# A fused attention and feed-forward kernel: the first four attention steps take the later steps' row halves, and their loads are cut and moved

## The chip, the cores and the metric

The kernel runs on one core of one Trainium2 chip, in one launch. The metric is device time in microseconds (us), the median of several executions; lower is better. The core's engines are TensorE (PE in the rows, its weight loads PEld), VectorE (DVE), ScalarE (ACT), GpSimd (POOL) and SyncE (SP), which issues nearly all the DMAs.

## The reference

Three stages run one after the other, all in float32:

```python
# 1. decayed linear attention, 2 batches, 8 heads, 768 positions in 12 blocks of 64, head size 64
for b in range(nb):
    qb, kb, vb = q[:, :, sl], k[:, :, sl], v[:, :, sl]
    intra = einsum('bhic,bhjc->bhij', qb, kb) * Dmask        # lam ** (i - j), lower triangle
    intra = einsum('bhij,bhjd->bhid', intra, vb)
    inter = einsum('bhid,bhde->bhie', qb * lam_pow, kv_state)
    out[:, :, sl] = intra + inter
    kv_state = lam_block * kv_state + einsum('bhsd,bhse->bhde', kb * rev_pow, vb)
# 2. x (1536 x 512): h = x @ w_in (512 x 2048); g = max(0.01 h, h); x = g @ w_out (2048 x 512)
# 3. h = x @ w_in2 (512 x 1024); softmax * h; layer norm * g_ln; @ w_out2 (1024 x 512)
```

## The kernel before

**Tiles of the attention.** The 12 blocks of 64 positions are steps 0 to 11. A step handles both batches (`NB` = 2) and four pairs of heads (`NPAIR` = 4); the two heads of a pair lie on the two halves of the 128 partitions. `HALF[h]` is rows 0 to 63 or 64 to 127, and `rows(h)` is the other half. A step has four groups of 64 x 64 matrix products, 16 products each (32 MATMUL rows in the profile, two for each):

- `scores_mm` (L204): k times q, into a bank; VectorE multiplies it with a decay table (`scores_ev`, L212) and gives `r`;
- `xs_mm` (L258): v times r, the part within the block;
- `state_mm` (L218): decayed k times v, which VectorE adds to the decayed state (`state_ev`, L244);
- `xq_mm` (L272): state times scaled q, accumulated with `xs_mm` in the same bank.

Here a quarter is the pair of the row half that a product's operands lie on and the row half of the bank that its result goes to. Before, the first `NPRE` = 4 steps keep k by position (`kj`) and v with head h on `HALF[h]` (`jrows`), and the later steps on `HALF[1 - h]`. So in steps 0 to 3 `scores_mm` and `xq_mm` both read `HALF[1 - h]` and write `HALF[h]`, which are the same two quarters, while `xs_mm` and `state_mm` have four different ones. Because the two parts of an x bank come from different row halves there, step 3 marks the banks with a small product and a copy (`see`, L249 to L252) between them, and the first `xq_mm` of steps 1 and 2 waits for the state's last addition by hand.

**The front.** The program runs steps 0 to 3 alone, up to the first product of the feed-forward part (`l1_mm`, L445), while it prepares the first weights. Each weight matrix (1 MB or 0.5 MB raw per half, `IN` and `OUT`) goes through two ScalarE passes (`words`: L358 and L362), three VectorE passes (`clamp` L368, `shift` L378, `join` L387), a ScalarE copy (`high` L415) and a VectorE subtraction (`low` L434). From then on TensorE alternates `l1_mm` (L445) and `l2_mm` (L461); its first `l2_mm` takes the result of the first `l1_mm` through two ScalarE instructions (L448, L451). Step 3's state product is left for later, and is paired with step 4's scores:

```python
            if i == 5:
                both(scores_mm, NPRE, aps[0], state_mm, NPRE - 1, kb)
```

(L1008; `both` puts two groups in turn, pair of heads by pair of heads.) Steps 4 to 11 follow inside the feed-forward loop, each with `both(xs, state)` and `both(xq, next scores)`.

**What sets the order.** Every engine runs its instructions in the order in which the code issues them; the last lines of the kernel chain them so. `load(queue, out, in_, limit)` lets a DMA start only when, with it, at most `limit` bytes are under way (2 MB by default, `AHEAD`; `CALM` is 1 MB), by a wait of the issuing queue for an older DMA. A DMA also waits for the one that used its semaphore before it; there are eight of these for SP and ACT together, in turn.

## Time and profile before

| | |
|---|---|
| median of 3 runs | 424.29 us (423.1 to 426.34) |
| the profiled execution | 423.9 us |
| its span, first to last instruction | 422.0 us |
| time outside the span | 1.9 us |
| TensorE busy | 413.6 us, 98% of the span |
| instructions in the profile | 8023 |

The span is from the first to the last instruction. A busy TensorE is not a TensorE at its peak, since matmuls are pipelined and their ends modelled. "Idle before, releaser" says how long an engine stood before an instruction and what ended the wait; "issue" is a wait for nothing that the profile shows.

### The profile page before, as it was taken

The page shows a single profiled execution, that of the slowest core. Times are in us where ns is not written, and L with a number is a line of the kernel's source. Part 1 is how long each engine was busy: PE and PEld are TensorE (multiplying, and loading weights), DVE is VectorE, ACT ScalarE, POOL GpSimd, SP SyncE. Part 2 cuts the span into 40 slices and gives each one's busy share as a digit, 9 for nine tenths or more (in the row PEclk, how much of TensorE's full clock was granted, in tenths as well). Part 3 has the DMA queues.
Part 4 walks back from the last instruction along what each step waited for, and adds up shares of the span by engine and source line. Part 5 has one row for each costly group of instructions (what it writes and reads, how often), then busy time and mean ns, then how long its engine had stood idle before and what let it go on. Part 6 is the DMA issues. An engine that isn't in the chain of part 4 may idle for free.

```text
span 422.0 us, 8023 instructions
## 1 busy us (share of the span) xinstructions
PE 413.6 (98%) x3166; PEld 340.4 (81%) x3166; DVE 323.7 (77%) x465; ACT 251.4 (60%) x395; POOL 126.0 (30%) x125
## 2 busy tenths in 40 slices
PE   7899999999999999999999999999999999999997
PEld 3778788888888888888888888888878888888886
DVE  4699999989894769988986789974569897847520
ACT  3598987867734555556465367742287558465621
POOL 0600001111157346236427342008212394123100
PEclk9999999999999999999999999999999999999999
DMA  8699995597300604413403745331043543535531
GB/s 294 246 319 364 311 346 165 159 272 223 109 23 1 214 37 149 127 49 125 149 29 122 236 148 190 100 101 26 2 143 106 161 158 107 182 120 173 176 123 51
DMA packets 30373, 64.69 MB, mean 153 GB/s; under 512 B 3328, under 2 KB 12032, under 8 KB 29824
## 3 DMA queue, kind: packets, MB, share of 16 engines
q1 hardware_dynamic: 30192, 63.79, 45.8%
q8 instruction: 25, 0.41, 0.4%
q10 hardware_dynamic: 144, 0.39, 0.3%
q14 instruction: 12, 0.10, 0.1%
HBM read 49.49 MB, written 14.68 MB: 152 GB/s over the span
## 4 chain that ended last, share of the span: by engine, by line
PE 84%; DMA 1%; DVE 1%; ACT 1%; issue 0%; SPq 0%; ACTq 0%
PE acc L461 19%; PE acc L676 11%; PE hps L445 9%; PE aps L795 8%; PE aps L560 8%; PE hps L560 8%; PE hps L795 7%; PE aps L461 5%; PE hps L461 5%; PE aps L258 2%; PE aps L272 1%; DMA lt<-kept_t 1%; PE hps L204 1%; DMA kept_t<-e 1%; PE aps L218 1%; ACT xhi L645 0%
## 5 line engine op out<-in xcount | busy, mean ns | idle before, releaser
L461 PE MATMUL acc<-ghi,wio 128*128 128x512 f32 x256 | 64.0, 392 | 0.3 <-DVE wio L434 0.3
L461 PEld LDWEIGHTS acc<-ghi,wio 128*128 128x128 f32 x256 | 47.6, 188 | 10.7 <-DVE wio L434 0.7
L445 PE MATMUL hps<-xhi,wio 128*128 128x512 f32 x160 | 42.1, 394 | 0.5 <-ACT xhi L307 0.5
L795 PE MATMUL aps<-wb,ln 128*128 128x512 f32 (+1 forms) x168 | 36.5, 375 | 0.1
L509 POOL TENSOR_TENSOR sw<-wio 128x512 f32<-128x512 f32 x14 | 21.9, 1582 | 46.7 <-DVE sj L528 46.7
L943 ACT ACTIVATE tf<-tf 128x512 f32<-128x512 f32 x28 | 17.7, 632 | 29.7 <-DVE tf L1121 29.7
L445 PEld LDWEIGHTS hps<-xhi,wio 128*128 128x128 f32 x160 | 29.6, 188 | 6.9 <-ACT xhi L307 0.6
L198 POOL TENSOR_TENSOR sd<-state,masks 128x512 f32<-128x512 f32 x9 | 9.6, 1063 | 85.0 <-DVE state L233 51.1
L795 PEld LDWEIGHTS aps<-wb,ln 128*128 128x128 f32 x168 | 29.9, 188 | 6.1 <-ACT ln L777 0.5
L461 PE MATMUL acc<-glo,wio 128*128 128x512 f32 x128 | 34.2, 389 | 0.0
L795 PE MATMUL hps<-wb,ln 128*128 128x512 f32 (+1 forms) x144 | 30.6, 371 | 0.0
L795 PEld LDWEIGHTS hps<-wb,ln 128*128 128x128 f32 x144 | 25.5, 188 | 4.8
L734 ACT ACTIVATE e<-e,small 128x1024 f32<-128x1024 f32 x12 | 13.8, 1150 | 25.1 <-DVE small L728 25.0
L461 PEld LDWEIGHTS acc<-glo,wio 128*128 128x128 f32 x128 | 24.0, 188 | 5.0
L362 ACT ACTIVATE raww<-raww 128x1024 uint32<-128x1024 uint16 (+1 forms) x28 | 27.8, 994 | 0.0
L676 PE MATMUL acc<-wa,xhi 128*128 128x512 f32 x104 | 27.8, 389 | 0.0
L358 ACT ACTIVATE x<-raww 128x1024 f32<-128x1024 f32 (+1 forms) x24 | 23.3, 969 | 7.0 <-DMA raww<-in_w_in_dram 7.0
L378 DVE SCALAR_TENSOR_TENSOR raww<-x,raww 128x1024 uint32<-128x1024 uint32 (+1 forms) x24 | 24.6, 1025 | 3.2 <-ACT raww L362 2.0
L781 DVE TENSOR_TENSOR ln<-lt,ln 128x1024 fp32r<-128x1024 f32 x12 | 15.3, 1273 | 14.0 <-ACT ln L777 14.0
L1121 DVE TENSOR_TENSOR tf<-aps,tf 128x512 f32<-128x512 f32 x26 | 17.6, 688 | 10.4 <-PE aps L560 10.0
L387 DVE SCALAR_TENSOR_TENSOR x<-x,raww 128x1024 uint32<-128x1024 uint32 (+1 forms) x24 | 24.8, 1032 | 0.1
L676 PEld LDWEIGHTS acc<-wa,xhi 128*128 128x128 f32 x104 | 19.4, 188 | 4.2 <-DVE e L714 0.2
(197 smaller groups left out, 998.2 us busy)
## 6 DMA issues: line engine op xcount, KB each, us to landing
raww<-in_w_out_dram SPq DMA_DIRECT2D x23, 512.0 KB, 5.1
raww<-in_w_in_dram SPq DMA_DIRECT2D x16, 512.0 KB, 5.6
kept_t<-e SPq DMA_DIRECT2D x12, 512.0 KB, 2.6
lt<-kept_t SPq DMA_DIRECT2D x48, 128.0 KB, 3.0
qk<-in_att_dram SPq DMA_DIRECT2D x8, 512.0 KB, 5.3
raww<-in_w_in_dram SPq DMA_DIRECT2D x4, 1024.0 KB, 5.1
gk<-kept_g SPq DMA_DIRECT2D x16, 256.0 KB, 2.7
kept_g<-tf SPq DMA_DIRECT2D x14, 256.0 KB, 2.0
```

Of the source, the lines that this page charges most:

```text
L358: act.activation(x, raw[:, :, 1].bitcast(F32), AF.Copy, scale=HI_SCALE)
L362: act.activation(raw[:, :, 0], raw.bitcast(U16)[:, :, 1], AF.Copy, scale=LO_SCALE)
L378: dve.scalar_tensor_tensor(raw[:, :, 0], x.bitcast(U32), 3, raw[:, :, 0], op0=ALU.logical_shift_left, op1=ALU.bitwise_or)
L387: dve.scalar_tensor_tensor(xu, xu, 0x80000000, raw[:, :, 0], op0=ALU.bitwise_and, op1=ALU.bitwise_or)
L445: pe.matmul(bank, w[:, s, k], x[b][:, k], start=(i == 0), stop=(i == len(terms) - 1))
L461: pe.matmul(banks[m], w[:, s, m], x, start=start, stop=stop)
L509: pool.tensor_tensor(t, w[:, 0], w[:, 1], op=ALU.add)
L560: pe.matmul(bank, left_[s][j], right[r][j], start=(i == 0), stop=(i == len(terms) - 1))
L676: pe.matmul(bank, x, Bp[w, j][:, s], start=(i == 0), stop=(i == len(terms) - 1))
L795: pe.matmul(po[:, 0:n], x[:, k], w2_t["b", k][:, s, cols], start=(i == 0), stop=(i == len(terms) - 1))
L943: act.activation(t, t if src is None else src, AF.Prelu, alpha=0.01)
L1121: dve.tensor_tensor(t, banks[n], other, op=ALU.add)
```

## The change

Only the first four steps and the loads ahead of the feed-forward part change:

- `kj` and v of steps 0 to 3 go to `rows(h)`, as in the later steps. Their loads are no longer part of two wide DMAs and one DMA for v, but two DMAs of 64 partitions for v and two for kj. A step is loaded by six DMAs (256 KB, 256 KB and four of 128 KB) where it was three (384, 384 and 256 KB).
- `scores_mm` of steps 0 to 3 writes `rows(h)`. The scores of steps 2 and 3 are issued in turn with `xq_mm` of steps 1 and 2 (`both`).
- `see`, its waits and the waits for the state's addition are gone.
- One decay table where there were two, so four scans fewer on VectorE.
- Step 3's `scale_k` is on GpSimd and not on ScalarE; `words`, `high`, `clamp`, `shift` and `join` of the first output weights stand in other places between steps 2 and 3 and the first `l1_mm`.
- The limit of the first output-side loads is 1.5 MB and 1 MB where it was 1.25 MB and 0.5 MB.

The line of the pairing at i == 5 is as before.

```diff
--- before.py
+++ after.py
@@ -74,9 +74,9 @@
     xlo = [cp.tile([P, KD, NBLK], F32R, name=f"xlo{i}") for i in range(NTOK // NBLK)]
 
 
-    masks = mp.tile([P, 3, NPAIR, CH], F32, name="masks")
-    dmask, dfirst, qpow = masks[:, 0], masks[:, 1], masks[:, 2]
-    junk = masks[:, 0:2].rearrange("p n a b -> p (n a b)").bitcast(BF16)
+    masks = mp.tile([P, 2, NPAIR, CH], F32, name="masks")
+    dmask, qpow = masks[:, 0], masks[:, 1]
+    junk = masks.rearrange("p n a b -> p (n a b)").bitcast(BF16)
     kept_y = dp.tile([KD, P, NBLK], F32, name="kept_y")
     kept_t = dp.tile([NTOK // P, P, FF2], F32, name="kept_t")
     kept_g = dp.tile([NF, P, NBLK], F32, name="kept_g")
@@ -89,14 +89,6 @@
     def rows(h):
 
         return HALF[1 - h]
-
-    def jrows(s, h):
-
-        return HALF[h] if s < NPRE else HALF[1 - h]
-
-    def decay(s):
-
-        return dfirst if s < NPRE else dmask
 
     def at(bank, rows, b, pr):
 
@@ -129,15 +121,29 @@
                 break
         flight.append((ins, size))
 
+    def put_kj(t, s):
+
+        for h in range(2):
+            load(sync, out=t[rows(h)], in_=att[2 * s : 2 * s + 2, HALF[h], 2].rearrange("n p a b -> p n a b"))
+
+    def put_v(t, s):
+
+        for h in range(2):
+            load(sync, out=t[rows(h)], in_=vt[s, HALF[h]])
+
     def load_step(s):
 
         t = wp.tile([P, 2048], F32, tag="w", name="ldw")
-        qkk = t[:, 0:1536].rearrange("p (n c a b) -> p n c a b", n=NB, c=3, a=NPAIR)
-        v = t[:, 1536:2048].rearrange("p (n a b) -> p n a b", n=NB, a=NPAIR)
+        qk = t[:, 0:1024].rearrange("p (n c a b) -> p n c a b", n=NB, c=2, a=NPAIR)
+        kj, v = (t[:, o : o + 512].rearrange("p (n a b) -> p n a b", n=NB, a=NPAIR) for o in (1024, 1536))
         for b in range(NB):
-            load(act if s + b == 1 and s == 0 else sync, out=qkk[:, b], in_=att[2 * s + b])
-        load(sync, out=v, in_=vt[s])
-        ld[s] = (qkk[:, :, 0], qkk[:, :, 1], qkk[:, :, 2], v)
+            load(act if s + b == 1 and s == 0 else sync, out=qk[:, b], in_=att[2 * s + b, :, 0:2])
+        ld[s] = (qk[:, :, 0], qk[:, :, 1], kj, v)
+
+    def load_kjv(s):
+
+        put_v(ld[s][V], s)
+        put_kj(ld[s][KJ], s)
 
     BOTH = slice(0, 2)
     qk_t = {}
@@ -152,16 +158,14 @@
         if s >= NS:
             return
         kj = ap1.tile(SHAPE, F32, tag="kj", name="kj")
-        for h in range(2):
-            load(sync, out=kj[rows(h)], in_=att[2 * s : 2 * s + 2, HALF[h], 2].rearrange("n p a b -> p n a b"))
+        put_kj(kj, s)
         ld[s][KJ] = kj
 
     def load_v(s):
         if s >= NS:
             return
         v = ap2.tile(SHAPE, F32, tag="v", name="v")
-        for h in range(2):
-            load(sync, out=v[rows(h)], in_=vt[s, HALF[h]])
+        put_v(v, s)
         ld[s] = {V: v}
 
     def scale_q(s, eng):
@@ -181,7 +185,7 @@
 
         if s >= NS - 1:
             return
-        kj, last = ld[s][KJ], decay(s)
+        kj, last = ld[s][KJ], dmask
         if eng is act:
             by_pair(kj, kj, last)
         else:
@@ -201,23 +205,21 @@
         q, k = (qk_t[s][:, :, 0], qk_t[s][:, :, 1]) if s >= NPRE else ld[s][0:2]
         for h in range(2):
             d = rows(h)
-            pe.matmul(at(bank, jrows(s, h), b, pr), k[d, b, pr], q[d, b, pr], start=True, stop=True)
+            pe.matmul(at(bank, d, b, pr), k[d, b, pr], q[d, b, pr], start=True, stop=True)
 
     def scores_ev(s, bank):
         if s >= NS:
             return
         r_t[s] = ap1.tile(SHAPE, F32, tag="r", name="r")
         for src, dst in parts(bank, r_t[s]):
-            mask = decay(s) if len(src.shape) == 3 else decay(s).unsqueeze(1).to_broadcast(SHAPE)
+            mask = dmask if len(src.shape) == 3 else dmask.unsqueeze(1).to_broadcast(SHAPE)
             dve.tensor_tensor(dst, src, mask, op=ALU.mult)
 
     def state_mm(s, bank, b, pr):
 
         for h in range(2):
-            j = jrows(s, h)
-            pe.matmul(at(bank, rows(h), b, pr), ld[s][KJ][j, b, pr], ld[s][V][j, b, pr], start=True, stop=True)
-
-    added = {}
+            j = rows(h)
+            pe.matmul(at(bank, j, b, pr), ld[s][KJ][j, b, pr], ld[s][V][j, b, pr], start=True, stop=True)
 
     def state_ev(s, bank):
         if s >= NS - 1:
@@ -230,54 +232,43 @@
         if s not in sd_t:
             src = bank.rearrange("p (n a b) -> p n a b", n=NB, a=NPAIR)
             for pr in range(NPAIR):
-                ins = dve.scalar_tensor_tensor(
+                dve.scalar_tensor_tensor(
                     s_t[s + 1][:, :, pr],
                     s_t[s][:, :, pr],
                     qpow[:, pr, CH - 1 : CH],
                     src[:, :, pr],
                     op0=ALU.mult,
                     op1=ALU.add,
-                ).ins
-                added.setdefault(s, ins)
+                )
             return
         for src, dst, old in parts(bank, s_t[s + 1], sd_t[s]):
-            added[s] = dve.tensor_tensor(dst, src, old, op=ALU.add).ins
-
-    LASTPRE, seen, mark = NPRE - 1, {}, tabs[:, 0:NB]
-
-    def see(s, b):
-        c = CH - 1
-        bank = (aps, hps)[b][0]
-        pe.matmul(bank[:, 0:CH], c1.to_broadcast([P, P]), c1.to_broadcast([P, CH]), start=True, stop=True)
-        seen[b] = act.copy(mark[:, b : b + 1], bank[:, c : c + 1]).ins
+            dve.tensor_tensor(dst, src, old, op=ALU.add)
+
+    LASTPRE = NPRE - 1
 
     def xs_mm(s, bank, b, pr):
 
         for h in range(2):
-            j = jrows(s, h)
-            ins = pe.matmul(
+            j = rows(h)
+            pe.matmul(
                 at(bank, HALF[h], b, pr),
                 ld[s][V][j, b, pr],
                 r_t[s][j, b, pr],
                 start=(s == 0 or (s != LASTPRE and pr + b == 0)),
                 stop=(s == 0 or (s == LASTPRE and pr == NPAIR - 1)),
-            ).ins
-            if s == LASTPRE and pr + h == 0:
-                tc.add_manual_dep(ins, seen[b].name, SYNC, reason="another half of rows")
+            )
 
     def xq_mm(s, bank, b, pr):
 
         for h in range(2):
             d = rows(h)
-            ins = pe.matmul(
+            pe.matmul(
                 at(bank, HALF[h], b, pr),
                 s_t[s][d, b, pr],
                 qs_t[s][d, b, pr],
                 start=(s == LASTPRE and pr == 0),
                 stop=(s != LASTPRE and pr + b == NPAIR + NB - 2),
-            ).ins
-            if s < LASTPRE and pr + b + h == 0:
-                tc.add_manual_dep(ins, added[s].name, SYNC, reason="another half of rows")
+            )
 
     def each_pair(*groups):
 
@@ -812,26 +803,30 @@
 
     pool.memset(one, 1.0)
     delta = heads(tabs[:, 0:256])
-    lams = tabs[:, 256:264].rearrange("p (a b) -> p a b", a=2)
+    lams = tabs[:, 260:264]
     pool.memset(zero, 0.0)
-    def scan(table, side, first):
+    def scan(table, first):
 
         for pr in range(NPAIR):
-            lam = lams[:, side, pr : pr + 1].to_broadcast([P, CH])
+            lam = lams[:, pr : pr + 1].to_broadcast([P, CH])
             if first is None:
                 dve.tensor_tensor_scan(table[:, pr], lam, delta[:, pr], 0.0, op0=ALU.mult, op1=ALU.add)
             else:
                 dve.tensor_tensor_scan(table[:, pr], lam, zero, first, op0=ALU.mult, op1=ALU.add)
 
     load(sync, out=tabs, in_=tab)
-    scan(dfirst, 0, None)
+    scan(dmask, None)
     load_step(0)
+    load_kjv(0)
     load_weights(0, IN)
     load_step(1)
+    load_kjv(1)
     load_step(2)
+    load_kjv(2)
     load_step(3)
-    load_weights(0, OUT, 5 * CALM // 4)
-    load_weights(1, OUT, CALM // 2)
+    load_kjv(3)
+    load_weights(0, OUT, 3 * CALM // 2)
+    load_weights(1, OUT, CALM)
     load_weights(2, BOTH, CALM)
     load_weights(3)
     load_qk(NPRE)
@@ -844,8 +839,7 @@
     scale_k(0, dve)
     busy(3)
     scores_ev(0, sb[0])
-    scan(qpow, 1, 1.0)
-    scan(dmask, 1, None)
+    scan(qpow, 1.0)
     scale_q(1, pool)
     words(0, IN)
     both(xs_mm, 0, xb[0], state_mm, 0, kb)
@@ -864,42 +858,35 @@
     join(0, IN)
     scale_q(2, pool)
     scale_k(2, act)
-    alone(scores_mm, 2, sb[0])
     state_ev(1, kb)
     decay_state(2, pool)
     high(0, IN)
-    alone(xq_mm, 1, xb[1])
+    both(xq_mm, 1, xb[1], scores_mm, 2, sb[0])
     scores_ev(2, sb[0])
+    x_hi(1, xb[1])
     low(0, IN)
-    x_hi(1, xb[1])
     both(xs_mm, 2, xb[0], state_mm, 2, kb)
+    scale_q(3, pool)
+    state_ev(2, kb)
     x_lo(1, xb[1])
-    scale_q(3, pool)
-    scale_k(3, act)
-
-    alone(scores_mm, 3, sb[1])
-    state_ev(2, kb)
     decay_state(3, pool)
-    word_hi(0, OUT)
-    alone(xq_mm, 2, xb[0])
+    scale_k(3, pool)
+    both(xq_mm, 2, xb[0], scores_mm, 3, sb[1])
+    words(0, OUT)
+    x_hi(2, xb[0])
     scores_ev(3, sb[1])
     clamp(0, OUT)
     x3 = (xb[1], hps[1])
-    for b in range(NB):
-        each_pair((xq_mm, 3, x3, b))
-        see(3, b)
-        if b == 0:
-            word_lo(0, OUT)
-            shift(0, OUT)
-    x_hi(2, xb[0])
-    join(0, OUT)
+    alone(xq_mm, 3, x3)
+    shift(0, OUT)
     x_lo(2, xb[0])
     alone(xs_mm, 3, x3)
+    join(0, OUT)
     x_hi(3, x3)
+    x_lo(3, x3)
+    words(1, OUT)
     high(0, OUT)
-    x_lo(3, x3)
     low(0, OUT)
-    words(1, OUT)
     clamp(1, OUT)
     shift(1, OUT)
     words(2, IN)
```

**TensorE, steps 2 and 3 up to the first feed-forward product.** L204 is `scores_mm`, L272 `xq_mm`, L251 `see`, L258 `xs_mm`, L445 `l1_mm`. Before, from the scores of step 3:

```order
L204 MATMUL acc_87<-ldw 64x64 x16
L272 MATMUL acc_84<-qs,state 64x64 x16
L272 MATMUL acc_85<-qs,state 64x64 x8
L251 LDWEIGHTS const-bfloat16-1.0
L251 MATMUL aps_90<-const-bfloat16-1.0 128x64
L272 MATMUL hps_89<-qs,state 64x64 x8
L251 LDWEIGHTS const-bfloat16-1.0
L251 MATMUL hps_88<-const-bfloat16-1.0 128x64
L258 MATMUL acc_85<-r,ldw 64x64 x8
L258 MATMUL hps_89<-r,ldw 64x64 x8
L445 MATMUL hps_88<-xhi_97,wio 128x512 x8
```

Now the first two groups stand in turn (the first rows of eight pairs of rows), L208 being `scores_mm`, L265 `xq_mm`, L253 `xs_mm` and L436 `l1_mm`:

```order
L265 MATMUL acc_84<-qs,state 64x64 x2
L208 MATMUL acc_87<-ldw 64x64 x2
...
L265 MATMUL acc_85<-qs,state 64x64 x8
L265 MATMUL hps_89<-qs,state 64x64 x8
L253 MATMUL acc_85<-r,ldw 64x64 x8
L253 MATMUL hps_89<-r,ldw 64x64 x8
L436 MATMUL hps_88<-xhi_97,wio 128x512 x8
```

The products of scores and xq alternate by twos, and no row of `see` is left between xq and xs of step 3.

**ScalarE, around x_hi of step 3.** L307 is `x_hi` (step 2, then step 3 in two halves), L358 and L362 are `words`, L415 `high`, L448 the activation after the first `l1_mm`. Before:

```order
L252 COPY tabs<-hps_88 128x1
L307 CAST xhi_97<-acc_84 128x2x4x64
L307 CAST xhi_97<-acc_85 128x4x64
L307 CAST xhi_97<-hps_89 128x4x64
L415 CAST wio<-x 128x512
L358 ACTIVATE x<-raww 128x512
L362 ACTIVATE raww<-raww 128x512
L358 ACTIVATE x<-raww 128x512
L362 ACTIVATE raww<-raww 128x512
L415 CAST wio<-x 128x512
L448 ACTIVATE hps_88<-hps_88 128x512
```

Now, with L298 `x_hi`, L349 and L353 `words`, L406 `high` and L439 the activation:

```order
L298 CAST xhi_97<-acc_84 128x2x4x64
L298 CAST xhi_97<-acc_85 128x4x64
L298 CAST xhi_97<-hps_89 128x4x64
L349 ACTIVATE x<-raww 128x512
L353 ACTIVATE raww<-raww 128x512
L406 CAST wio<-x 128x512
L349 ACTIVATE x<-raww 128x512
L353 ACTIVATE raww<-raww 128x512
L406 CAST wio<-x 128x512
L439 ACTIVATE hps_88<-hps_88 128x512
```

The first `high` after `x_hi` stood ahead of the two `words` of the next weights, and now stands behind them.

**SP, the loads of the first two steps.** Each row is one DMA or several alike, in the order of issue. Before:

```order
L123 DMA tabs<-in_tab_dram 128x264
L123 DMA ldw<-in_att_dram 128x768
L123 DMA ldw<-in_vt_dram 128x512
L123 DMA raww<-in_w_in_dram 128x1024
L123 DMA ldw<-in_att_dram 128x768 x2
L123 DMA ldw<-in_vt_dram 128x512
```

Now:

```order
L115 DMA tabs<-in_tab_dram 128x264
L115 DMA ldw<-in_att_dram 128x512
L115 DMA ldw<-in_vt_dram 64x512 x2
L115 DMA ldw<-in_att_dram 64x2x256 x2
L115 DMA raww<-in_w_in_dram 128x1024
L115 DMA ldw<-in_att_dram 128x512 x2
L115 DMA ldw<-in_vt_dram 64x512 x2
L115 DMA ldw<-in_att_dram 64x2x256 x2
```

The bytes per step are the same; k by position, which came within the first two DMAs of a step, now comes last.

## Rows read from the trace of the kernel before

**Rows 1.** The page: busy time of each engine, its share of the span, and instructions

```profile
PE 413.6 (98%) x3166; PEld 340.4 (81%) x3166; DVE 323.7 (77%) x465; ACT 251.4 (60%) x395; POOL 126.0 (30%) x125
```

**Rows 2.** Stages: length; busy PE, PEld, DVE, ACT, POOL; granted clock; DMA share; GB/s

```profile
0.00:25.00 25.00, 20.01 (x476) 14.69 (x477) 14.94 (x33) 13.11 (x30) 7.38 (x12) 1.00 0.78 265
25.00:45.00 20.00, 20.00 (x89) 16.31 (x87) 18.78 (x33) 17.59 (x30) 0.00 (x0) 1.00 0.99 344
45.00:65.00 20.00, 19.71 (x145) 16.05 (x145) 19.64 (x23) 18.19 (x26) 0.00 (x0) 1.00 0.98 347
```

**Rows 3.** Waits of TensorE in the first 120 us: total, times, longest

```profile
PE acc L204 <- DMA ldw<-in_att_dram: 2.0, 2, 1.1
PE acc L204 <- issue: 1.7, 2, 1.5
PE acc L461 <- DVE wio L434: 0.3, 1, 0.3
```

**Rows 4.** Timeline of TensorE, steps 0 to 3: start, length, what, idle before

```profile
8.18 0.23 PE L258 MATMUL acc<-r,ldw 64*64 64x64 f32 x2
...
13.12 0.52 PE L204 MATMUL acc<-ldw 64*64 64x64 f32 x12
13.86 0.74 PE L204 MATMUL acc<-ldw 64*64 64x64 f32 x19 [0.23 <-issue]
...
16.44 0.52 PE L204 MATMUL acc<-ldw 64*64 64x64 f32 x12
18.42 0.80 PE L204 MATMUL acc<-ldw 64*64 64x64 f32 x20 [1.46 <-issue]
19.05 1.57 PE L272 MATMUL acc<-qs,state 64*64 64x64 f32 x48
20.55 0.20 PE L251 MATMUL aps<-const-bfloat16-1.0 128*128 128x64 bf16 x1
20.68 0.68 PE L272 MATMUL hps<-qs,state 64*64 64x64 f32 x16
```

**Rows 5.** The page's queue of instruction fetches: packets, MB, share

```profile
q8 instruction: 25, 0.41, 0.4%
```

**Rows 6.** Two stages of the front, columns as in Rows 2

```profile
10.00:15.00 5.00, 4.09 (x134) 3.33 (x136) 3.13 (x5) 2.54 (x9) 3.51 (x3) 1.00 0.99 359
15.00:20.00 5.00, 3.54 (x151) 3.40 (x147) 3.39 (x6) 3.06 (x8) 3.50 (x4) 1.00 0.42 142
```

**Rows 7.** TensorE: first and last of 64 rows, scores of step 4 with state of 3

```profile
45.06 0.27 PE L204 MATMUL aps<-qk 64*64 64x64 f32 x2
...
45.99 0.22 PE L218 MATMUL aps<-ldw 64*64 64x64 f32 x2
```

**Rows 8.** Timeline from the first l1_mm to the first l2_mm

```profile
23.05 2.11 PE L445 MATMUL hps<-xhi,wio 128*128 128x512 f32 x8 [0.47 <-ACT xhi L307]
23.52 0.66 ACT L358 ACTIVATE x<-raww 128x512 f32<-128x512 f32 x1
24.08 0.66 ACT L362 ACTIVATE raww<-raww 128x512 uint32<-128x512 uint16 x1
24.14 0.68 DVE L434 TENSOR_TENSOR wio<-x,wio 128x512 fp32r<-128x512 f32 x1
26.71 0.62 ACT L415 CAST wio<-x 128x512 fp32r<-128x512 f32 x1 [0.39 <-DVE x L387]
28.64 1.98 PE L461 MATMUL acc<-ghi,wio 128*128 128x512 f32 x8
```

**Rows 9.** DMAs by line: count, KB each, median us to landing

```profile
ldw<-in_att_dram SPq DMA_DIRECT2D x7, 384.0 KB, 5.6
kj<-in_att_dram SPq DMA_DIRECT2D x16, 128.0 KB, 4.0
```

**Rows 10.** The queue of SP: issue of the load of step 1's v

```profile
5.83 0.43 SPq L123 DMA_DIRECT2D ldw<-in_vt_dram  x1
```

**Rows 11.** GpSimd: scaled q of step 3, freed by that step's load

```profile
16.39 1.37 POOL L173 TENSOR_TENSOR qs<-ldw,masks 128x512 f32<-128x512 f32 x1 [0.31 <-DMA ldw<-in_att_dram]
```

## The prediction

> **What bounds the kernel now.** I read the page first: TensorE is busy for 413.6 us of the 422.0 us span [rows 1]. Then the stages: in the first 25 us it is busy for 20.01 us, from 25 to 45 us for all 20.00, and from 45 to 65 for 19.71 [rows 2]. So an edit pays if it lets the dense part start sooner or makes the dense part shorter, and an edit of the front also pays only as far as VectorE and ScalarE follow: they are busy for 18.78 and 17.59 of 20 us there, and VectorE for 19.64 of the 20 after it. The granted clock is 1.00 in all of these, so it plays no part. The waits of TensorE say what stretches the front: 2.0 us for the loads of the attention, and 1.7 us in two gaps that nothing shown ends ("issue"), 1.5 of it in one piece [rows 3].
>
> The timeline shows these two gaps, 0.23 us before 13.86 and 1.46 before 18.42, both after 12 rows of a step's scores [rows 4]. I read them as TensorE waiting for its own instructions. Between 13.86 and the second gap stand 20 rows of scores, 32 of xq, 64 of xs and state and 12 of scores: 128 products, with as many weight loads 256 instructions. The page has a queue of 25 instruction fetches [rows 5], and TensorE's 2 x 3166 instructions [rows 1] divided by 25 are 253. The data is no explanation: q and k of step 3 were there at 16.39 [rows 11], two us before the products went on. [...] From 13.86 to 18.42 is 4.56 us, with the DMA engines' share at 0.99 until 15 and 0.42 after it [rows 6]; the entry before that, 128 products earlier, lies at 8.18 [rows 4], 5.68 us before 13.86 and in a stretch of full DMA.
>
> **The change, part by part.** All sums are against the profiled execution, 423.9 us.
>
> *Two groups in turn, no marks.* Products of one group alone, on two quarters, come every (1.57 - 0.22) / 47 = 0.029 us [rows 4]. Two groups on four quarters come every (45.99 - 45.06) / 62 = 0.015 us [rows 7]. TensorE's instruction count up to the scores of step 2 hardly moves, so I expect the gaps at the same counts: after 12 of the 64 rows of xq 1 and scores 2, and again, 128 products on, after 12 of the 64 of xq 2 and scores 3. Behind the second gap stand 52 x 0.015 = 0.78, xq of step 3 32 x 0.029 = 0.93, xs 0.93, the last product's 0.22, and the copy up to the first l1_mm, 0.48 as now: 3.3 us. Before, it was 23.05 - 18.42 = 4.63 [rows 4, 8]; about half of the difference is the shared quarters, half the marks and the copies between. Term: **-1.3 us**. The same edit in step 2, between the gaps, gains nothing if the gaps stay: TensorE then only waits longer.
>
> *Where the second gap ends.* No row shows it for the new loads. k by position now comes last of a step's six pieces, some 256 KB after where it came; at 359 GB/s [rows 6] that is up to 0.7 us for step 1's k, of which the decay table's product on VectorE covers a part, so TensorE enters the block at 14.1 rather than 13.86 (my estimate). [...] From below: entry at 13.86 and a fetch shorter by the 0.4 us that fewer bytes under way might give, 18.0. From above: 14.1 + 5.68 = 19.8. I take 19.05, nearer the 4.56 row because the load falls off in the middle here too: **+0.6 us**, ends -0.4 and +1.4.
>
> *Order on ScalarE.* Now the high of the first output weights starts as soon as x_hi ends, and the low on VectorE at 24.14 is held by VectorE alone; 2.57 us after that the next high begins (26.71), and the first l2_mm 1.93 us after it [rows 8]. With the change the two words (23.52 to 24.74, 1.22 us) stand between x_hi and high. From the end of the gap: x_hi ends at 3.25, words at 4.5, high (0.62) at 5.1, so low begins at 5.1, the next high at 7.7, and l2_mm at 9.65. Before, it was 28.64 - 18.42 = 10.22. So l2_mm gains 0.57 where l1_mm gains 1.3: a new wait of TensorE, **+0.7 us**. From below 0, if VectorE's part is shorter than now since its x_lo is done earlier; not above 0.7, since the words are all that is put in.
>
> *The pairing at i == 5.* This line is not edited, but its quarters are. Before, scores 4 lies on rows and banks `HALF[1 - h]`, state 3 goes from `HALF[h]` to `HALF[1 - h]`: four quarters, and the 64 rows show 0.015 us each [rows 7]. Now state 3 reads `HALF[1 - h]` too, so both use the same two quarters, and I price them like a group alone: 64 x (0.029 - 0.015) = 0.9 us, in the dense part. VectorE isn't held, so the 0.3 us that TensorE waits for it a little later [rows 3] goes: **+0.6 us**. Ends: 0, and 0.9.
>
> *Covered.* Four scans fewer on VectorE end before step 1's loads allow the next work, and so gain nothing. Step 3's scale_k moves to GpSimd, with nothing to do from 25 us on [rows 2], and is needed at 45; without that cover it would cost about one instruction of 1.4 us [rows 11]. On ScalarE its four instructions leave a place where ScalarE then waits for weights anyway. The 12 added DMAs take 12 x 0.43 = 5.2 us of SP [rows 10]; SP stands waiting for older DMAs most of that time, and what it costs if not is the slow rival below.
>
> Sum: -1.3 + 0.6 + 0.7 + 0.6 = +0.6, so 424.5 us on the scale of the profiled execution. That one lies 0.4 below the median of its three runs, which spread over 3.2 us; I say **424.7 us** for the median, half of that offset.
>
> **The rivals.**
>
> *Faster.* The second gap ends as now or sooner, and VectorE, done with x_lo earlier, makes up half of the new wait: -1.3 + 0 + 0.35 + 0.6 = -0.35 with the gap at 18.42, and -0.75 with it at 18.0: 423.2 to 423.6 us. For it: only eight DMAs can be under way, 8 x 171 KB = 1.4 MB where 2 MB were. Against: bytes and rate are the same, and the looser limits fill just the pause in which the fetch landed.
>
> *Slower: the loads run dry.* Eight pieces of 171 KB on average per time to landing: at the 5.6 us of now [rows 9] that is 244 GB/s where 359 flow [rows 6], and the 3.1 MB of steps 1 to 3 take 12.9 instead of 8.8 us, 4.1 more; at the 4.0 us of the 128 KB pieces [rows 9] it is 342 GB/s and 0.4 us more. It decides once step 3's q and k land after the second gap's end, 2.3 us later than the 16.39 of now. At worst 1.8 us are left over: 424.5 + 1.8 = 426.3 us. Against: fewer bytes under way also land sooner.
>
> *The gaps are no fetch.* Then xq 2 and scores 3 start when step 2 is through, at about 17.0, and the first l1_mm could follow 3.5 us later; but x_hi of step 2 now stands behind the words of the first output weights, which land at about 18.5, so l1_mm starts near 21.2, 1.85 sooner than 23.05. With the terms for l2_mm and the pairing: -1.85 + 0.7 + 0.6 = -0.55, 423.3 us. The traces speak against it, by the count of 256. [...]
>
> **How the numbers follow.** The forecast 0.5 (its own range 423.5 to 425.5), faster 0.22, loads run dry 0.2, no fetch 0.08. The range leaves out the upper end of the dry loads and the largest gains: 422.8 to 426.3. A change under 1% (4.2 us) can't be told from none for this kernel with few runs that spread so; no case reaches it, so same gets 0.94, faster 0.03, slower 0.03.
>
> **What would show it.** After: no row of see; xq and scores of a step 0.015 us apart; an "issue" gap of TensorE inside xq 2 and scores 3 that ends near 19; the first l1_mm 3.3 us after it, and a wait of ScalarE's or VectorE's making before the first l2_mm; scores 4 and state 3 in 1.9 us where it was 0.95. I am wrong if the gaps are gone, if the pairing still takes 0.95, or if step 3's q lands after 18.5.

## The result, and the profile after

The changed kernel takes 429.66 us (median of 4 runs, 428.99 to 430.12) beside 423.7 us for the kernel before on the same chip (4 runs, 422.53 to 426.34): ratio 1.0131, 95% interval [1.0102, 1.0161]. It is slower by 1.3%; the forecast was 424.7 us, in a range that ended at 426.3. The profiled execution's span is 427.7 us where it was 422.0, so 5.7 us have to be found.

The page of the kernel after, as in [rows 1]:

```profile
PE 415.8 (97%) x3163; PEld 342.0 (80%) x3164; DVE 322.7 (75%) x461; ACT 249.6 (58%) x389; POOL 127.2 (30%) x126
```

TensorE is busy 2.2 us longer with three instructions fewer, so part of the 5.7 us is slower work and the rest is idle time. The stages, columns as in [rows 2]:

```profile
0.00:25.00 25.00, 18.39 (x461) 12.66 (x464) 9.85 (x21) 7.29 (x17) 8.45 (x13) 0.86 0.80 217
25.00:45.00 20.00, 18.10 (x83) 14.74 (x79) 18.06 (x33) 17.24 (x31) 0.09 (x1) 0.91 0.92 338
45.00:65.00 20.00, 20.00 (x144) 16.55 (x144) 19.25 (x23) 16.82 (x21) 0.00 (x0) 1.00 1.00 317
...
10.00:15.00 5.00, 4.27 (x81) 2.78 (x73) 2.02 (x5) 2.17 (x4) 1.77 (x2) 0.55 1.03 226
15.00:20.00 5.00, 4.20 (x157) 3.42 (x156) 2.55 (x4) 2.45 (x8) 2.85 (x3) 0.77 0.79 222
```

Three things differ from [rows 2, 6]. TensorE is idle longer in the first 45 us (8.5 us where it was 5.0). From 10 to 15 us the DMA engines are as busy as before (share 1.03, before 0.99) but move 226 GB/s where they moved 359. And the granted clock, 1.00 before, is 0.55 and 0.77 in two stages, so a "busy" TensorE does less there: its 32 rows of scores at 12.05, at a clock of 0.50, take 2.18 us, and the 32 at 4.70, at 1.00, took 1.15.

Waits of TensorE in the first 120 us, total, times, longest, against [rows 3]:

```profile
PE acc L253 <- DVE r L216: 3.7, 2, 2.9
PE hps L436 <- ACT xhi L298: 1.9, 1, 1.9
PE acc L265 <- issue: 1.3, 1, 1.3
...
PE acc L208 <- DMA ldw<-in_att_dram: 0.6, 2, 0.4
```

The loads of the attention stood first there by name; now they stand behind VectorE's and ScalarE's names. The timelines show it: first a row of VectorE and one of ScalarE of the kernel before, then TensorE, VectorE, GpSimd and ScalarE of the kernel after (start, length, what, idle before and releaser).

```profile
5.57 0.69 DVE L188 TENSOR_TENSOR ldw<-ldw,masks 128x512 f32<-128x512 f32 x1 [0.53 <-DMA ldw<-in_att_dram]
19.12 0.67 ACT L358 ACTIVATE x<-raww 128x512 f32<-128x512 f32 x1 [1.51 <-DMA raww<-in_w_in_dram]
```

```profile
8.13 0.69 DVE L192 TENSOR_TENSOR ldw<-ldw,masks 128x512 f32<-128x512 f32 x1 [3.50 <-DMA ldw<-in_att_dram]
8.74 0.68 DVE L216 TENSOR_TENSOR r<-acc,masks 128x512 f32<-128x512 f32 x1
9.48 0.27 PE L253 MATMUL acc<-r,ldw 64*64 64x64 f32 x2 [2.87 <-DVE r L216]
...
20.99 1.48 POOL L177 TENSOR_TENSOR qs<-ldw,masks 128x512 f32<-128x512 f32 x1 [1.43 <-DMA ldw<-in_att_dram]
22.34 0.27 PE L265 MATMUL acc<-qs,state 64*64 64x64 f32 x1 [1.25 <-issue]
24.91 0.67 ACT L349 ACTIVATE x<-raww 128x512 f32<-128x512 f32 x1 [3.81 <-DMA raww<-in_w_in_dram]
26.05 0.84 ACT L298 CAST xhi<-acc 128x512 fp32r<-128x512 f32 x2
26.78 0.38 ACT L298 CAST xhi<-hps 128x256 fp32r<-128x256 f32 x1
27.21 3.52 PE L436 MATMUL hps<-xhi,wio 128*128 128x512 f32 x8 [1.90 <-ACT xhi L298]
34.41 1.98 PE L452 MATMUL acc<-ghi,wio 128*128 128x512 f32 x8
```

VectorE waits for step 0's k by position, so its product with the decay table starts at 8.13 (5.57 before); `scores_ev` follows it, and TensorE stands behind both. Step 3's q and k free GpSimd at 20.99, 4.60 us later than in [rows 11]. The first output weights land some 5.8 us later than before (the words, which wait for them, start at 24.91 and not at 19.12), and x_hi of steps 2 and 3 stand behind their words on ScalarE. So the first `l1_mm` starts at 27.21, 4.16 later than in [rows 8]. After its wait TensorE runs at a granted clock of 0.50, from 27.5 to 30.9: its first eight products take 3.52 us where they took 2.11. The first `l2_mm` is 5.77 later than before (34.41, 28.64). That is the whole 5.7 us; what follows about cancels out.

The pairing at i == 5 in the kernel after, first and second row of a group, the last, and the `l1_mm` behind it, against [rows 7]:

```profile
50.82 0.33 PE L208 MATMUL aps<-qk 64*64 64x64 f32 x4
50.98 0.28 PE L222 MATMUL aps<-ldw 64*64 64x64 f32 x4
...
52.62 0.28 PE L222 MATMUL aps<-ldw 64*64 64x64 f32 x4
52.83 1.19 PE L436 MATMUL hps<-xhi,wio 128*128 128x512 f32 x4
```

Up to that `l1_mm` it takes 2.01 us where it took 1.18 (45.06 to 46.24): 0.029 us per row instead of 0.015.

Issue of DMAs by SP in the kernel after, then the loads by line as in [rows 9]:

```profile
1.16 0.42 SPq L115 DMA_DIRECT2D ldw<-in_att_dram  x1
1.63 1.18 SPq L115 DMA_DIRECT2D ldw<-in_vt_dram  x2
2.86 1.30 SPq L115 DMA_DIRECT2D ldw<-in_att_dram  x2
...
16.93 1.13 SPq L115 DMA_DIRECT2D ldw<-in_vt_dram  x2
18.11 1.29 SPq L115 DMA_DIRECT2D ldw<-in_att_dram  x2
19.51 0.52 SPq L115 DMA_DIRECT2D raww<-in_w_in_dram  x1
```

```profile
ldw<-in_att_dram SPq DMA_DIRECT2D x7, 256.0 KB, 6.3
ldw<-in_vt_dram SPq DMA_DIRECT2D x8, 128.0 KB, 5.3
ldw<-in_att_dram SPq DMA_DIRECT2D x8, 128.0 KB, 4.8
```

A pair of DMAs of 64 partitions takes SP 1.13 to 1.30 us in these rows, 0.57 to 0.65 each, not the 0.43 of [rows 10] (one by one they range from 0.49 to 0.66; DMAs of 128 partitions mostly take 0.33 to 0.43 here, and at times 0.59). From 16.93 on SP issues them back to back. A piece of 256 KB now needs 6.3 us to land, where 384 KB needed 5.6.

### The profile page after: what moved, and what is told of

Same layout as the page of the kernel before. It is cut to its first block, busy times and chain, and to the rows that moved or that the text cites. A ratio compares the mean times of both kernels' runs of the same rounds, so it can differ in the third digit from the quotient of the medians.

```text
span 427.7 us, 8025 instructions
## 1 busy us (share of the span) xinstructions
PE 415.8 (97%) x3163; PEld 342.0 (80%) x3164; DVE 322.7 (75%) x461; ACT 249.6 (58%) x389; POOL 127.2 (30%) x126
## 4 chain that ended last, share of the span: by engine, by line
PE 90%; DMA 4%; SPq 3%; ACT 1%; DVE 1%; issue 0%; ACTq 0%
PE acc L452 21%; PE hps L436 13%; PE acc L667 10%; PE aps L786 8%; PE aps L551 8%; PE hps L551 8%; PE hps L786 7%; PE hps L452 5%; PE aps L452 5%; SPq L115 2%; DMA ldw<-in_att_dram 2%; PE aps L253 2%; PE aps L265 1%; DMA raww<-in_w_in_dram 1%; DMA lt<-kept_t 1%; PE aps L222 1%
## 5 line engine op out<-in xcount | busy, mean ns | idle before, releaser
L436 PE MATMUL hps<-xhi,wio 128*128 128x512 f32 x160 | 43.5, 404 | 1.9 <-ACT xhi L298 1.9
L436 PEld LDWEIGHTS hps<-xhi,wio 128*128 128x128 f32 x160 | 30.4, 193 | 8.5 <-ACT xhi L298 2.0
L349 ACT ACTIVATE x<-raww 128x1024 f32<-128x1024 f32 (+1 forms) x24 | 23.2, 969 | 12.5 <-DMA raww<-in_w_in_dram 12.5
L353 ACT ACTIVATE raww<-raww 128x1024 uint32<-128x1024 uint16 (+1 forms) x28 | 28.0, 1000 | 0.0
```

What stands on the lines that cost most here:

```text
L349: act.activation(x, raw[:, :, 1].bitcast(F32), AF.Copy, scale=HI_SCALE)
L353: act.activation(raw[:, :, 0], raw.bitcast(U16)[:, :, 1], AF.Copy, scale=LO_SCALE)
L436: pe.matmul(bank, w[:, s, k], x[b][:, k], start=(i == 0), stop=(i == len(terms) - 1))
```

## The experiments

Theories, named by a letter in the texts on record: **H**, DMAs that cover only 64 partitions move slowly; **P**, the number of pieces counts, whatever they cover; **C**, the granted clock carries the loss; **R**, the new order of ScalarE and TensorE in the front does. Ratios are to the kernel before, with 95% intervals.

**The change with wide loads.** The host stores k by position and v with the head halves exchanged, so that each step loads as before, in three DMAs of 128 partitions, while all else of the change stays.

```diff
-            load(act if s + b == 1 and s == 0 else sync, out=qk[:, b], in_=att[2 * s + b, :, 0:2])
+            load(act if s + b == 1 and s == 0 else sync, out=qkk[:, b], in_=att[2 * s + b])
+        load(sync, out=v, in_=vt[s])
-        put_v(ld[s][V], s)
-        put_kj(ld[s][KJ], s)
```

> The change with one thing taken back: k by position and v of steps 0 to 3 come as before, within two DMAs of 384 KB and one of 256 KB on all 128 partitions (the arrays in device memory hold them with the heads' halves exchanged, so no copy is needed). Theory H (loads on 64 partitions move slowly): the cumulated bytes are as before, step 0's k lands before 6.2 us, TensorE does not stand 2.9 us before 9.5, the granted clock stays 1.00, and the first l1_mm starts between 21.5 and 23; 423 to 425 us. Theory P (too many pieces for eight DMAs under way): the same, since the pieces are gone too. Rival R (the loss lies in the new order of the work, not in the loads): stays at 428 us or more.

Measured: 423.52 us, ratio 0.9991 [0.9973, 1.0008]; span 422.6. The loss is gone, so R falls. Two stages, waits of TensorE, and its timeline at the first `l1_mm` and `l2_mm`:

```profile
5.00:10.00 5.00, 4.22 (x117) 2.91 (x117) 3.25 (x8) 2.09 (x4) 0.00 (x0) 1.00 1.00 341
10.00:15.00 5.00, 3.57 (x128) 2.61 (x132) 2.83 (x4) 1.50 (x6) 2.37 (x3) 1.00 1.01 378
```

```profile
PE acc L452 <- ACT ghi L442: 1.2, 1, 1.2
PE acc L253 <- DVE r L216: 0.8, 1, 0.8
...
PE acc L208 <- issue: 0.7, 1, 0.7
```

```profile
21.68 2.14 PE L436 MATMUL hps<-xhi,wio 128*128 128x512 f32 x8 [0.49 <-ACT xhi L298]
...
29.02 2.11 PE L452 MATMUL acc<-ghi,wio 128*128 128x512 f32 x8 [1.19 <-ACT ghi L442]
```

The rate is back, the clock is 1.00, the wait for `r` is 0.8 us. The first `l1_mm` starts at 21.68, 1.37 sooner than before; yet the first `l2_mm` is at 29.02, 0.38 later, after a new wait of 1.19 us for ScalarE. (The profiled execution took 424.41 us, 0.9 us over the median of its kernel.)

**The kernel before with the cut loads**, and nothing else of the change (the pieces go to its own halves):

```diff
+        for b in range(NB):  # q, k
+            load(..., out=qk[:, b], in_=att[2 * s + b, :, 0:2])
+        for h in range(2):
+            load(sync, out=v[HALF[h]], in_=vt[s, HALF[h]])
+        for h in range(2):
+            load(sync, out=kj[HALF[h]], in_=att[2 * s : 2 * s + 2, HALF[h], 2]...)
```

> The kernel before with the loads of steps 0 to 3 alone cut as in the change: q and k in two DMAs of 256 KB, v and k by position in two DMAs of 64 partitions each, to the same row halves as before; all else as before. H and P: the whole loss and more, 428 to 431 us, since the front of before gives nothing back. R: 423 to 425 us.

Measured: 428.73 us, ratio 1.0117 [1.0087, 1.0148], nearly all of the loss. Its stages from 10 to 20 us, at a clock of 1.00:

```profile
10.00:15.00 5.00, 4.38 (x118) 2.81 (x113) 4.28 (x10) 2.80 (x7) 2.53 (x2) 1.00 1.07 252
15.00:20.00 5.00, 4.03 (x144) 3.50 (x144) 1.38 (x2) 1.58 (x5) 2.28 (x2) 1.00 0.98 234
```

From 10 to 15 us the DMA engines, as busy as in the kernel before (share 1.07, there 0.99), move 252 GB/s where they moved 359 [rows 6], so C isn't needed for most of the loss. The first `l1_mm` started at 26.23. The profiled execution, at a clock of 1.00, took 427.12 us, 0.9% over the kernel before; the other three, at a mean clock of 0.995 to 0.996, took 428.49 to 429.35. So the clock may hold a further 0.3%, which so few executions do not show.

**As many pieces, all of 128 partitions**: v and k by position cut by batch, not by rows, in runs of 1 KB (the host exchanges the head halves here too).

```diff
-        put_v(ld[s][V], s)
-        put_kj(ld[s][KJ], s)
+        for b in range(NB):
+            load(sync, out=ld[s][V][:, b], in_=vt[s, :, b])
+        for b in range(NB):
+            load(sync, out=ld[s][KJ][:, b], in_=att[2 * s + b, :, 2])
```

> The change with its six pieces per step, in the same order and of the same sizes, but v and k by position cut by batch, so that each piece covers all 128 partitions (1 KB runs). H: the bytes flow as before or nearly so (about 350 GB/s from 5 to 10 us), the first l1_mm starts before 23.5, 423 to 425.5 us. P: as slow as the change, 428 us or more, since the number of DMAs and the eight under way are the same.

Measured: 425.08 us, ratio 1.0040 [1.0018, 1.0062]; 301 and 316 GB/s from 5 to 15 us (H had expected about 350), and the first `l1_mm` at 23.40. So P has a price, about 0.5% over the wide loads, but 0.9% of the change's 1.4% needs the 64 partitions. Nor do pieces of 128 partitions keep SP as long: in the kernel after they mostly take it 0.33 to 0.43 us, and those of 64 partitions 0.49 to 0.66. So no run here parts slow transfer of 64 partitions from their slower issue: with the engines full from 10 to 15 us the transfer is what shows, from 16.93 to 19.51 us the issue may add to it.

**One operand in halves at a time**, from the kernel with wide loads:

```diff
-        load(sync, out=v, in_=vt[s])
+        put_v(v, s)
```

> The change with q, k and k by position in wide DMAs and v alone in two DMAs of 64 partitions (2 KB runs, five DMAs less per front than the change has more). Theory H: the 2 KB packets of the 64-partition DMAs take longer than the 84 ns of wide ones, the rate from 5 to 10 us falls between 341 (wide) and 272 GB/s (all in halves), and half the loss returns: 425 to 427 us. If only the 1 KB runs of k by position are slow: 423.5 to 424.5 us.

Measured: 425.55 us, ratio 1.0040 [1.0020, 1.0061]. The time is in H's range, about a third of the loss and not half; but the rate from 5 to 10 us, which H had falling, was 347 GB/s and did not fall. The longest wait of TensorE ahead of the first `l1_mm` (22.46) was here a gap of 1.52 us, an "issue" gap like those of [rows 4], that ended at 19.01. Whether v in halves made it longer is not shown.

```diff
-            load(..., out=qkk[:, b], in_=att[2 * s + b])
+            load(..., out=qkk[:, b, 0:2], in_=att[2 * s + b, :, 0:2])
+        put_kj(qkk[:, :, 2], s)
```

> The kernel with wide loads (e1_wide, 0.9991 of before), but k by position of steps 0 to 3 alone in two DMAs of 64 partitions after v; v stays in one DMA of 128 partitions. 64-partition loads are slow (H): v alone in halves cost 0.5% over e1_wide, the change with both in halves 1.4%, so k in halves costs more than v, because its runs are half as long (1 KB): about 0.9%, ratio 1.006 to 1.009, 5 to 10 us at 290 to 310 GB/s, the first l1_mm at 23 to 26. If it is the number of pieces (P): five pieces against six with all partitions (1.0040): ratio 1.001 to 1.004, l1_mm near 22.5.

Measured: 427.24 us, ratio 1.0082 [1.0060, 1.0104], as H had it and outside P's range; the first `l1_mm` at 24.70. Over the wide loads v costs 0.49% and k 0.91%; together with the 0.9991 they give 1.0131, the change's ratio, though each of them is uncertain by some 0.2% and includes the price of its added pieces. The stage from 10 to 15 us with v, and then with k, in halves:

```profile
10.00:15.00 5.00, 3.83 (x147) 2.80 (x145) 2.84 (x5) 1.84 (x7) 2.56 (x3) 1.00 1.04 326
```

```profile
10.00:15.00 5.00, 3.23 (x52) 1.81 (x55) 3.28 (x5) 3.01 (x7) 2.28 (x2) 1.00 0.99 243
```

**Filler products for the clock**, in the changed kernel:

```diff
-    busy(3)
+    busy(16)  # after the scores of step 0
...
+    busy(8)  # ahead of the first l1_mm
```

> The change with small products on constants put where TensorE stood idle (13 more after step 0's scores, 8 before the first l1_mm), which fall into the waits, so that TensorE does not stand still; nothing else. Theory C (the halved clock after the idle stretches carries the loss): the clock stays 1.00 and 2 to 4 us come back, 425.5 to 427.5 us. H or P alone: the loads still set the front, the first l1_mm stays near 27, and only its first 8 products gain (about 1.4 us): 428 to 428.5 us.

Measured: 429.04 us, ratio 1.0141 [1.0098, 1.0184], no gain. The filler held the clock at 1.00 up to 15 us, but not from 15 to 25 (0.72 and 0.60). The first `l1_mm` ran at a clock of 1.00, its eight products in 2.20 us, but started at 28.20, behind the filler; the first `l2_mm` was at 33.87, 0.54 sooner than in the changed kernel, and the runs don't resolve that. Since the clock did not stay at 1.00 as C's expectation needed, what C is worth below 0.4% stays open.

**ScalarE's order under late loads**: in the changed kernel, x_hi of step 2 ahead of the words that wait for the first output weights.

```diff
-    words(0, OUT)
     x_hi(2, xb[0])
+    words(0, OUT)
```

> The kernel after, its cut loads kept, with x_hi of step 2 ahead of the two words of the first output weights on ScalarE. In the trace of after these words wait 3.81 us for their load, until 24.91, and x_hi of steps 2 and 3 stand behind them, so the first l1_mm starts at 27.21, 1.90 after TensorE's last product. If a part of the late load's price comes through this order: only x_hi of step 3 stays behind the words (26.05), so the first l1_mm starts near 26.7 and the first l2_mm is nearer to the chain of the weights; ratio 1.011 to 1.013, at most 0.1% better than 1.0131, because the words themselves, their shift, high and low still set the first l2_mm. If ScalarE's order is what the late loads are paid through: l1_mm near 25.8, ratio 1.009 to 1.010.

Measured: 428.41 us, ratio 1.0132 [1.0104, 1.0159]: no gain, the first of the two expectations. (The profiled execution, of 431.68 us, had the first `l1_mm` at 27.48, at a clock of 0.50, where 26.7 was expected.) The late loads are paid for in either order.

**The terms under the loads.** From the kernel with wide loads, `high` and `low` of the first output weights stand ahead of the next words, as before the change:

```diff
     x_hi(3, x3)
-    x_lo(3, x3)
-    words(1, OUT)
     high(0, OUT)
+    x_lo(3, x3)
     low(0, OUT)
+    words(1, OUT)
```

> The change with the loads on 128 partitions, and high and low of the first output weights back ahead of the words of the next weights, as in the kernel before; nothing else. By the prediction's term for ScalarE's order the wait before the first l2_mm (1.19 us in the run with wide loads) shrinks by about 0.7 and the time with it: 422.8 us. If the wait comes from the landing of the next output weights (22.95 us) rather than from the order, l2_mm moves by 0.3 us at most: 423.2 to 423.5.

Measured: 422.94 us, ratio 0.9979 [0.9962, 0.9996]; span 420.5. It is the only kernel here whose interval lies below 1. TensorE at the first `l1_mm` and `l2_mm`:

```profile
21.20 2.14 PE L436 MATMUL hps<-xhi,wio 128*128 128x512 f32 x8 [0.97 <-ACT xhi L298]
...
27.27 2.11 PE L452 MATMUL acc<-ghi,wio 128*128 128x512 f32 x8 [0.30 <-ACT ghi L442]
```

The wait before `l2_mm` is 0.30 instead of 1.19 us, and `l2_mm` starts 1.75 sooner. That is in the profiled executions, of 422.28 and 424.41 us; in the ratios the order is worth 0.1%, which the two intervals don't resolve.

**State 3 paired in the front**, not at i == 5, with scale_k of step 3 on ScalarE (from the kernel with wide loads, and then with the order above too):

```diff
-    alone(xs_mm, 3, x3)
+    both(xs_mm, 3, x3, state_mm, 3, kb)
...
-                both(scores_mm, NPRE, aps[0], state_mm, NPRE - 1, kb)
+                alone(scores_mm, NPRE, aps[0])
```

> The change with the loads on 128 partitions (as the earlier run that gave 423.5 us), and step 3's state product moved from the pairing with step 4's scores to the front, in turn with step 3's xs, which lies on the other two quarters; step 4's scores then stand alone, and step 3's scale_k is on ScalarE as before. If two groups on the same two quarters cost TensorE double (0.9 us in the trace of the change), this takes 0.9 us out of the dense part: 422.6 to 422.9 us, less if VectorE was the bound behind the pairing. If the pairing was free for the end, 423.5.

> Both edits of the two runs beside this one, on the change with wide loads. If the terms add: 1.0 to 1.6 us less than with wide loads alone, 421.9 to 422.5 us, and below the kernel before (ratio 0.996 to 0.998). If VectorE bounds the part behind, the second edit adds nothing and it equals the better of the two.

Measured: 424.81 us, 1.0037 [1.0018, 1.0057], and with the order 424.06 us, 1.0017 [0.9997, 1.0038]. Both are about 0.4% slower than their counterparts, where both expectations had them faster or equal. The gap of TensorE in the first of them, and its scores of step 4, now alone:

```profile
22.00 0.27 PE L253 MATMUL hps<-r,ldw 64*64 64x64 f32 x1 [1.95 <-issue]
22.96 1.65 PE L436 MATMUL hps<-xhi,wio 128*128 128x512 f32 x3 [0.40 <-ACT xhi L298]
...
46.34 1.15 PE L208 MATMUL aps<-qk 64*64 64x64 f32 x32
```

Thirty-two more rows stand in the front, and a gap of 1.95 us now falls right ahead of the first `l1_mm`, which starts at 22.96 where it was 21.68. What the pairing saved later (the scores take 1.07 us up to the next `l1_mm`, at 47.41, where the pair took 2.01) was spent here. In this profile the clock was also at 0.50 from 22.5 to 25.9 (0.75 and 0.91 in the stages of 5 us from 20 to 30); with the order too it stayed at 1.00, and the gap was 1.66 us.

**Two more edits on the fastest kernel.** The first puts the limits of the first output-side loads back:

```diff
-    load_weights(0, OUT, 3 * CALM // 2)
-    load_weights(1, OUT, CALM)
+    load_weights(0, OUT, 5 * CALM // 4)
+    load_weights(1, OUT, CALM // 2)
```

> The fastest kernel so far (e7_order, 0.9979) with the limits of the first output-side loads back at 1.25 MB and 0.5 MB. If the looser limits brought something: the words of the second output weights wait longer for their load, the first l2_mm at 27.8 or later (27.27 with the looser limits), ratio 0.999 to 1.000. If they brought nothing or hurt the loads of step 3: l2_mm at 27.0 to 27.4, ratio 0.996 to 0.998. By words(1) standing behind low in this order, I expect nothing: 0.998.

Measured: 423.04 us, 0.9985 [0.9968, 1.0001]; beside 0.9979 no difference can be told. (Its profile had the first `l2_mm` at 28.17, not at the expected 27.0 to 27.4, but there an "issue" gap of 1.48 us had put `l1_mm` off to 22.60, and no wait stood before `l2_mm`; it says nothing on the limits.) The second takes x_hi of step 2 ahead of the words, as above:

> The fastest kernel so far (e7_order, 0.9979) with x_hi of step 2 ahead of the words of the first output weights. There the words land at 18.89, and l1_mm waits 0.97 us for x_hi. If x_hi alone sets the start: l1_mm near 20.7 (21.20), l2_mm and the end 0.3 to 0.5 us sooner, ratio 0.9967 to 0.9975. If the chain of weights through words, VectorE and high sets the first l2_mm (27.27): the wait moves from before l1_mm to before l2_mm, ratio 0.998. I expect the second.

Measured: 422.99 us, 0.9994 [0.9979, 1.0009]. The wait before `l1_mm` fell to 0.5 us, and the one before `l2_mm` grew to 0.40, with `l2_mm` at 27.28, as expected where the chain of the weights sets it.

## Why the prediction was wrong, point by point

**The step that failed** is "Covered", with the rate behind it. The prediction took the rate of the wide loads, 359 GB/s [rows 6], for pieces that cover 64 partitions, so that k was late by "up to 0.7 us", and held the 12 added DMAs hidden in SP's idle time. In the kernel after, the DMA engines are full (share 1.03) at 226 GB/s from 10 to 15 us; SP needs 0.49 to 0.66 us for each such DMA; q and k of step 3 are 4.60 us late, the first output weights 5.8. At 226 GB/s the 3.1 MB of steps 1 to 3 take 13.9 us where the prediction had 8.8; this estimate of 5.1 us more is the size of what was measured. The prediction's own sign of error, step 3's q after 18.5, came true at 20.99.

The traces show what the partitions cost: 226 and 222 GB/s in the two stages from 10 to 20 us (shares 1.03 and 0.79), where four of a step's six pieces, half of its bytes, cover 64 partitions; from 10 to 15 us it is 359 in the kernel before, and 316 (share 0.98) with as many pieces of 128 partitions. The prediction weighed bytes and pieces, and not the partitions that a piece covers.

**"The loads run dry"** was the right rival with the wrong mechanism and price. It had 244 GB/s at worst and too few bytes under way; from 10 to 15 us the engines were not dry but full (share 1.03), at 226. In the next stage they did run low (share 0.79; 0.39 from 15 to 16 us). Its better price, 342 GB/s, came from the 4.0 us of [rows 9]; those DMAs cover 64 partitions too, but the row tells the time of one to landing and not the rate of a queue full of them. It also let 2.3 of the 4.1 us vanish in the slack behind the second gap, and counted q and k only. The first output weights, behind them in the queue, had no such slack: words, x_hi and `l1_mm` hang on them.

**The other terms** can be read in the kernel with wide loads. Its span is 0.6 us over the span before, which is the prediction's sum, but by chance: that execution took 0.9 us more than the median, and the ratio (0.9991) shows no loss. One by one:

- Two groups in turn: from the last gap to the end of xs of step 3 the prediction had 52 x 0.015 + 0.93 + 0.93 + 0.22 = 2.86 us; in the kernel after it is 2.97 (22.34 to 25.31). Right, but there x_hi then waited for the words.
- The second gap's end: expected at 19.05, 0.6 later than before, and at 18.0 at the earliest; with wide loads it ended at 17.77, 0.65 sooner. Wrong in sign: the gap was all but gone (under 0.1 us of TensorE, where the first was 0.73), 3.56 us after the first one's end. The first `l1_mm` at 21.68 came close to the rival without a fetch (21.2): xs ended at 21.18, and ScalarE, without a pause since the words began at 19.37, started the last x_hi at 21.23, so either could have set it. With the order of before, where xs ended at 20.22 and `l1_mm` waited 0.97 us for x_hi, the words did.

```profile
14.21 0.27 PE L208 MATMUL acc<-ldw 64*64 64x64 f32 x2 [0.73 <-issue]
...
17.77 0.27 PE L208 MATMUL acc<-ldw 64*64 64x64 f32 x2
```

- Order on ScalarE: a new wait before the first `l2_mm`, expected 0.7 us at most, measured 1.19 with wide loads, and 0.30 with the old order. Right in place, and too small: the words of the next weights also waited 1.35 us for their load. The changed kernel has no such wait; there TensorE, at a clock of 0.50 up to 30.9, took 7.20 us from the first `l1_mm` to the first `l2_mm` (5.59 before).
- The pairing: expected +0.9 on the same two quarters, measured 2.01 - 1.18 = +0.83. VectorE's wait of 0.3 went, as expected. Right.
- The granted clock, which "plays no part", did: the eight products of the first `l1_mm` took 1.41 us longer at a clock of 0.50.

**The gaps as fetches** held up, though not their length: in the kernel after, too, the crossings of TensorE's count by 256 lie at 17.51 and 22.34, the second with the gap; and where 32 rows were put ahead, a gap fell ahead of the first `l1_mm`, at 22.00, 256 instructions behind one at 17.32. The packets of the instruction queue fit: one of 16 KB ran from 11.62 to 12.61 and one from 15.67 to 16.97 in the kernel before, one from 19.71 to 20.93 in the kernel after, and a gap ended 1.3 to 1.4 us behind each. The gaps reach 1.95 us, the longest with the rows put ahead, beside 1.46 in the kernel before. When a fetch is asked for, which the prediction's 4.56 and 5.68 us for the second gap's end need, no run shows: in the kernel before, the packets began at 11.62, 15.67 and 19.56, which is 3.4, 1.8 and 1.1 us behind 8.18, 13.86 and 18.42, and not at one distance.

## What to carry to other kernels

Price a load by the partitions that it covers, and not only by its bytes (here 226 GB/s where 359 flowed): if data must change its row half, let the host's layout do it, and keep the DMA at 128 partitions (here 423.52 us where the cut loads took 429.66). When a load is late, follow it to the items behind it in its queue; here the last one that the front waits for had the least slack. A shorter TensorE front pays only up to the next engine's chain: here 1.37 us at `l1_mm` were lost again before `l2_mm` in the profile, until `high` stood ahead of the next words.

## What the hardware showed

- In the kernel after, the granted clock fell at 10.5, behind an idle stretch of TensorE of 2.87 us (6.61 to 9.48), to 0.50, until 17.3; behind one of 1.90 us it was at 0.50 from 27.5 to 30.9. With filler products in the first idle stretch the fall at 10.5 was gone, and one came at 17.2 (0.72 from 15 to 20 us), inside a gap of 1.87 us. The length of the stretch alone doesn't tell: in the kernel before with the cut loads TensorE stood for 2.25 us, and the clock stayed at 1.00.
- Up to 14 us in the changed kernel, packets of 1 KB, which its pieces of 64 partitions have, took a median of 73 ns; those of 1056 bytes of the first load, on 128 partitions, took 47. By an estimate from the first number, sixteen engines at 1 KB per 73 ns would move 224 GB/s; from 10 to 15 us the trace has 226, and that of the run with as many pieces of 128 partitions 316. Packets of 2 KB took a median of 84 ns in the kernel before. With v alone in halves 326 GB/s flowed from 10 to 15 us, and 378 with wide loads.
